# Rewriting a fused S4-convolution, dense-SiLU forward and backward kernel: feature-major FFN with DMA transposes, per-channel SSM columns, data-stationary inverse DFT, natural-layout gradients

## The chip, the cores and the metric

The kernel runs on one core of one Trainium2 chip. Times are microseconds (us) of device time for one execution, as medians over several runs; smaller is better. The profile is one execution of the kernel, and its span differs a little from the median. Engines are named as the profile names them: PE (matmul), PEld (weight load; its busy time overlaps PE's, 161 beside 190 us in the 268 us of SSM forward below), DVE (VectorE), ACT (ScalarE), POOL (GpSimd), SP (the SyncE queue that issues DMAs). An eviction is a copy of a matmul's result from PSUM to SBUF, and a DMA's landing is the arrival of its data, counted here from its issue.

## The reference, cut to what matters

The program computes the forward pass and all gradients of `x + s * g`, with sequence length L = 2048, model width D = 512, state N = 128, FFN width F = 1792, all in bfloat16.

```python
xn = layernorm(x)                                   # [2048, 512]
# branch A: S4 convolution
P  = exp(dt * A * l)                                # [512, 128, 2048], never stored whole
K  = real(einsum("dn,dnl,dn->dl", C, P, dt * B))    # one kernel of 2048 taps per channel
s  = irfft(rfft(xn, 2L) * rfft(K, 2L))[:L] + xn * Dskip
# branch B: gate
g  = silu(silu(xn @ w1) @ w2)                       # [2048, 512] @ [512, 1792] @ [1792, 512]
out = x + s * g
# ... and the gradients with respect to x, A, B, C, log_dt, Dskip, w1, w2, given grad_out
```

Both kernels work in the same stages, whose letters are used below. (A) setup, layernorm, FFN forward and tables of exponentials. (B) SSM forward: the kernel taps K are built from products of these tables, 32 chunks of 16 channels. (C) convolution by DFT on PE, four blocks of 128 channels. (D) backward of FFN and SSM. (E) weight gradients (dW2, dW1) and the last parameter gradients.

## The kernel before: the parts that matter

SSM forward, one chunk (cut): two strided evictions of the taps, with a mask, and a sum of both later; then K goes to DRAM and is read back by the convolution.

```python
ps = psum.tile([P, 8, 32, 2], F32, name="ps_k", tag="ps")
# ... 32 matmuls ...
nc.scalar.activation(out=tmpP[:, 1, :, qa:qa + 8].rearrange("p j q -> p q j"), in_=ps[:, :, :, 1], func=ACT.Copy, scale=k.odd[:, 0:1])
nc.scalar.activation(out=tmpP[:, 0, :, qa:qa + 8].rearrange("p j q -> p q j"), in_=ps[:, :, :, 0], func=ACT.Copy, scale=k.even[:, 0:1])
# ... after all chunks of a block ...
nc.vector.tensor_tensor(out=KF[:], in0=tmpP[:, 0], in1=tmpP[:, 1], op=ALU.add)
```

Inverse DFT (cut): a stage, then PE transposes with their own evictions, then the second stage.

```python
for g0 in range(0, G, 4):
    # ... matmuls with the DFT matrix as the stationary operand ...
    EV(nc, Z[:, c, g0:g0 + 4, :], ps[:])
for c in range(2):
    for g0 in range(0, G, 8):
        # ... 8 PE transposes of Z into pt ...
        EV(nc, dst, src)
# ... second stage ...
```

The FFN backward works token by token and rebuilds what it needs (cut):

```python
for t in range(T):
    # dO of this token tile, transposed on PE (pt_do)
    for fc in range(NFC):
        # ps_h: h again, 4 matmuls; ps_da: 4 matmuls
        nc.scalar.activation(out=a_s[:, fs], in_=ps_h[:], func=ACT.Silu)
        nc.scalar.activation(out=th[:], in_=ps_h[:], func=ACT.Tanh, scale=0.5)
        # ... three DVE operations for silu' ...
        nc.vector.scalar_tensor_tensor(out=dh_s[:, fs], in0=u[:], scalar=1.0, in1=ps_da[:], op0=ALU.add, op1=ALU.mult)
    nc.sync.dma_start(k.Ad[t], a_s[:])
    # ... 14 PE transposes of dh_s (pt_dh), dhT evicted, ps_dx ...
```

The stages follow one another: `gen_half` (tables) beside the FFN forward, then SSM forward, then the convolution, then the backward, then the weight gradients beside the final SSM gradients. DMAs alternate between the queues of SP and ACT.

## Time and profile before

The median is 1345 us (four runs, 1341.65 to 1346.33). The view below gives, for each stretch of the span (us), the busy time of each engine with the number of its instructions, the clock granted to PE, the busy share of the DMA engines and their rate. The stretches are the stages: setup; FFN and tables (A); SSM forward (B); convolution (C); backward (D); weight gradients and finish (E).

```profile
core 0: us, PE busy (x) PEld busy (x) DVE busy (x) ACT busy (x) POOL busy (x), PEclk, DMA share, GB/s
0.00:56.00 56.00, 10.75 (x56) 5.91 (x58) 25.29 (x55) 37.33 (x74) 5.91 (x42) 1.00 0.22 78
56.00:255.00 199.00, 108.32 (x501) 49.44 (x510) 133.85 (x194) 154.81 (x206) 3.45 (x8) 0.80 0.30 109
255.00:523.00 268.00, 190.26 (x2704) 161.04 (x2704) 241.01 (x390) 160.41 (x219) 0.00 (x0) 0.84 0.49 153
523.00:850.00 327.00, 211.96 (x1936) 135.66 (x1956) 202.01 (x220) 186.88 (x299) 0.00 (x0) 0.87 0.27 60
850.00:1170.00 320.00, 243.62 (x1975) 137.04 (x1995) 229.38 (x530) 166.88 (x337) 0.00 (x0) 0.86 0.78 177
1170.00:1348.00 178.00, 128.19 (x1087) 91.47 (x1091) 62.90 (x104) 37.92 (x83) 0.00 (x0) 0.82 0.69 160
```

Read each row for its busiest engine. SSM forward keeps DVE busy 241 of 268 us. The convolution keeps no engine busy for more than 65% of its 327 us: its engines wait for each other much of the time. So a change that runs these two beside each other has room: their DVE sums, for example, are 443 us in 595.

The groups of instructions (line, engine, operation, out<-in, shapes; then busy us and mean ns; then the idle time before them and what ended it) that the change removes or replaces, among others:

```profile
L646 ACT ACTIVATE kf_tmpP<-ps_k,even 128x256 bf16<-128x256 f32 x32 | 51.8, 1619 | 5.5 <-DVE YTf L634 5.5
L645 ACT ACTIVATE kf_tmpP<-ps_k,odd 128x256 bf16<-128x256 f32 x32 | 45.4, 1420 | 78.0 <-PE ps_k L642 76.5 <-PE ps_s_5496 L105 0.8 <-PE pf_t L621 0.6
L770 DVE TENSOR_TENSOR Gbd<-Gt,MK 128x512 bf16<-128x512 bf16 x64 | 43.4, 687 | 37.5 <-PE psV L777 36.0 <-DMA Gt<-dKd 1.5
L902 ACT ACTIVATE b_th<-ps_hb 128x448 bf16<-128x448 f32 x64 | 34.7, 542 | 0.0
```

### The profile page before, as it was taken

How to read it: one execution, taken by the hardware profiler on the slowest of the kernel's cores; microseconds unless marked ns; L12 is line 12 of the kernel's file. 1: busy time of each engine (PE TensorE's matmuls, PEld its weight loads, DVE VectorE, ACT ScalarE, POOL GpSimd, SP SyncE). 2: the span in 40 equal slices, each digit the busy share in tenths (PEclk: the TensorE clock that was granted, in tenths of full speed). 3: DMA queues.
4: the chain of work that ended last, by engine and by line, in shares of the span. 5: the costliest groups of instructions: out<-in, count | busy, mean ns of one | idle time of the engine just before them, and what ended most of it. 6: DMA issues, size and time to landing. Idle time of an engine off the chain costs nothing. (4 is left out here: it accounts for less than half of the span.)

```text
span 1348.3 us, 20797 instructions
## 1 busy us (share of the span) xinstructions
PE 893.1 (66%) x8258; PEld 580.6 (43%) x8314; DVE 894.4 (66%) x1490; ACT 744.2 (55%) x1217; POOL 9.4 (1%) x50
## 2 busy tenths in 40 slices
PE   1486850376767674666676666288788888646997
PEld 0232320266656563334354443144444444333487
DVE  7177877597989894494756748187777777857100
ACT  5779887285646455547475565255555555541111
POOL 0000000000000000000000000000000000000000
PEclk9999985587888887889898888598888898856999
DMA  3112312546463736442411102977686877897744
GB/s 129 59 62 86 133 67 89 206 158 210 125 195 103 204 110 146 97 94 47 94 33 32 32 1 46 221 160 184 150 185 153 178 168 180 156 171 211 176 130 117
DMA packets 333686, 171.90 MB, mean 127 GB/s; under 512 B 287890, under 2 KB 300052, under 8 KB 333076
## 3 DMA queue, kind: packets, MB, share of 16 engines
q1 hardware_dynamic: 179348, 102.65, 28.5%
q10 hardware_dynamic: 154240, 67.91, 20.3%
q8 instruction: 65, 1.06, 0.3%
q14 instruction: 33, 0.27, 0.1%
HBM read 93.19 MB, written 77.33 MB: 126 GB/s over the span
## 5 line engine op out<-in xcount | busy, mean ns | idle before, releaser
L620 PE MATMUL pf_t<-ident_bfloat_87,Xc 128*128 128x128 bf16 x512 | 84.4, 247 | 96.1 <-DVE Xc L344 72.9
L620 PEld LDWEIGHTS <-Xc 128*128 128x128 bf16 x512 | 54.3, 112 | 80.6 <-issue 69.9
L645 ACT ACTIVATE kf_tmpP<-ps_k,odd 128x256 bf16<-128x256 f32 x32 | 45.4, 1420 | 78.0 <-PE ps_k L642 76.5
L622 ACT CAST XTf<-pf_t 128x512 bf16<-128x512 f32 x128 | 74.0, 658 | 26.1 <-PE pf_t L621 12.5
L779 ACT CAST Vb<-psV 128x512 bf16<-128x512 f32 x128 | 67.1, 594 | 29.8 <-PE psV L777 23.3
L621 PE MATMUL pf_t<-ident_bfloat_87,Xc 128*128 128x128 bf16 x512 | 79.3, 245 | 4.2 <-DVE Xc L347 3.5
L922 PE MATMUL ps_dx<-W1T,dhT 128*128 128x512 bf16 x204 | 66.4, 472 | 7.0 <-ACT dhT L184 4.7
L770 DVE TENSOR_TENSOR Gbd<-Gt,MK 128x512 bf16<-128x512 bf16 x64 | 43.4, 687 | 37.5 <-PE psV L777 36.0
L621 PEld LDWEIGHTS <-Xc 128*128 128x128 bf16 x512 | 54.1, 112 | 31.9 <-issue 23.0
L524 PE MATMUL ps_h<-XNT,W_291 128*128 128x512 bf16 x217 | 55.8, 407 | 16.8 <-ACT th L538 9.5
L899 PE MATMUL ps_da<-W2T,DOT_s 128*128 128x448 bf16 x256 | 60.9, 358 | 7.8 <-ACT DOT_s L184 3.7
L633 PE MATMUL pt_t<-ident_bfloat_87,YY 128*64 128x128 bf16 x512 | 49.0, 252 | 23.5 <-DVE YY L331 14.1
L896 PE MATMUL ps_hb<-W_291,XNT 128*128 128x448 bf16 x256 | 60.7, 355 | 3.1 <-ACT Vb L779 1.9
L642 PE MATMUL ps_k<-YY,Xc 128*128 128x64 bf16 x1024 | 48.8, 207 | 15.4 <-ACT kf_tmpP L646 14.8
L646 ACT ACTIVATE kf_tmpP<-ps_k,even 128x256 bf16<-128x256 f32 x32 | 51.8, 1619 | 5.5 <-DVE YTf L634 5.5
L534 PE MATMUL ps_o<-W_440,aT 128*128 128x512 bf16 x220 | 49.8, 379 | 4.8 <-ACT aT L526 4.5
L633 PEld LDWEIGHTS <-YY 128*64 128x64 bf16 x512 | 38.3, 129 | 33.2 <-DVE YY L331 17.5
L777 PE MATMUL psV<-XT,Gbd 128*128 128x256 bf16 x256 | 48.6, 330 | 5.8 <-DVE Gbd L770 2.6
L642 PEld LDWEIGHTS <-Xc 128*128 128x128 bf16 x1024 | 42.8, 107 | 21.2 <-issue 16.9
L974 PEld LDWEIGHTS <-xn 128*128 128x128 bf16 x512 | 48.9, 98 | 4.1 <-issue 2.2
L114 PE MATMUL pt_b<-ident_bfloat_87,dftA 128*128 128x128 bf16 x384 | 31.5, 238 | 28.3 <-ACT dftA L26 14.8
L634 DVE COPY YTf<-pt_t 64x1024 bf16<-64x1024 bf16 x64 | 41.8, 680 | 11.9 <-PE pt_t L633 7.3
(2228 smaller groups left out, 2558.9 us busy)
## 6 DMA issues: line engine op xcount, KB each, us to landing
XTD<-XTf SPq DMA_DIRECT2D x32, 512.0 KB, 3.3
XT<-XTD SPq DMA_DIRECT2D x32, 512.0 KB, 4.3
YTD<-YTf ACTq DMA_DIRECT2D x32, 256.0 KB, 2.9
YT<-YTD SPq DMA_DIRECT2D x32, 256.0 KB, 4.0
YT<-YTD ACTq DMA_DIRECT2D x32, 256.0 KB, 4.8
Ad<-a_s SPq DMA_DIRECT2D x16, 448.0 KB, 3.3
DHd<-dh_s ACTq DMA_DIRECT2D x16, 448.0 KB, 4.3
A_ft<-Ad SPq DMA_DIRECT2D x7, 512.0 KB, 4.0
```

What stands on the lines that cost most here:

```text
L524: nc.tensor.matmul(out=ps[:], lhsT=W1[:, dk, ft * P:(ft + 1) * P], rhs=XNT[:, dk, 4 * tcn:4 * tcn + 4, :], start=(dk == 0), stop=(dk == DK ...
L534: nc.tensor.matmul(out=pso[:], lhsT=aT[:, ft, tt * P:(tt + 1) * P], rhs=W2[:, ft, :], start=(ft == 0), stop=(ft == FT - 1))
L620: nc.tensor.matmul(out=pf[:, qi, c, :], lhsT=X[:, 2 * c, qb + qi].rearrange("p a b -> p (a b)"), rhs=k.ident[:], start=True, stop=False)
L621: nc.tensor.matmul(out=pf[:, qi, c, :], lhsT=X[:, 2 * c + 1, qb + qi].rearrange("p a b -> p (a b)"), rhs=k.ident[:], start=False, stop=True)
L622: nc.scalar.copy(out=XT[:, qb:qb + 2], in_=pf[:])
L633: nc.tensor.transpose(out=pt[0:64, qi, c, :], in_=YY[:, c, qb + qi, 0:32, :].rearrange("p j e -> p (j e)"), identity=k.ident[:])
L642: nc.tensor.matmul(out=ps[:, qi].rearrange("p j e -> p (j e)"), lhsT=X[:, m, q].rearrange("p a b -> p (a b)"), rhs=YY[:, m // 2, q, 32:64, ...
L646: nc.scalar.activation(out=tmpP[:, 0, :, qa:qa + 8].rearrange("p j q -> p q j"), in_=ps[:, :, :, 0], func=ACT.Copy, scale=k.even[:, 0:1])
L779: nc.scalar.copy(out=Vb[:, qb:qb + 2], in_=psV[:])
L896: nc.tensor.matmul(out=ps_h[:], lhsT=XNT[:, dk, t, :], rhs=W1[:, dk, fs], start=(dk == 0), stop=(dk == DK - 1))
L899: nc.tensor.matmul(out=ps_da[:], lhsT=DOT_s[:, dk, :], rhs=W2T[:, dk, fs], start=(dk == 0), stop=(dk == DK - 1))
L922: nc.tensor.matmul(out=ps_dx[:], lhsT=dhT[:, ft, :], rhs=W1T[:, ft, :], start=(ft == 0), stop=(ft == FT - 1))
```

## The change

The intent: keep the FFN feature-major (features on partitions), so that the backward needs no recomputed h; fetch transposed operands by DMA transpose instead of PE; run SSM forward of block b beside the convolution of block b-1; make the data the stationary operand in the inverse DFT, which saves its transposes; sum the SSM gradients with a fixed stationary selector; do the final gradients in natural layout. Nearly the whole file changes; the core, cut:

```diff
 # stage order
-        interleave([gen_half(k), gf], [1, 6])
-        interleave([gen_ssm_fwd(k, (hp, ck)), ffn_then_wT()], [2, 1])
+    interleave([half, gf], [1, 2])
+        run(gen_ssm_fwd(k, 0))
+        for b in range(1, NB):
+            interleave([gen_ssm_fwd(k, b), gen_conv(k, b - 1)], [1, 2])
+        run(gen_conv(k, NB - 1))
 # ...
 # tables: one single-buffered tile T4, its copies on GpSimd
+    T4 = hp.tile([P, 2, HSZ], BF16, name="T4")
+        for h in range(2):
+            nc.gpsimd.tensor_copy(out=vXH[:, h, 0:2, :, :, 1], in_=vXH[:, h, 0:2, :, :, 0])
+            nc.gpsimd.tensor_copy(out=vYL[:, h, :, :, 1]..., in_=vYL[:, h, :, :, 0]...)
+            nc.gpsimd.tensor_copy(out=yh[:, :, 1], in_=yh[:, :, 0])
+            nc.gpsimd.tensor_scalar(out=T4[:, h, OXH + 2048:OYL], in0=T4[:, h, OXH + 1024:OXH + 2048], scalar1=-1.0, ...)
+        nc.sync.dma_start(k.hd[:, 2 * b:2 * b + 2, :], T4[:])
 # ...
 # taps: no mask, no sum, K stays in SBUF
-                nc.scalar.activation(out=tmpP[:, 1, ...].rearrange("p j q -> p q j"), in_=ps[:, :, :, 1], func=ACT.Copy, scale=k.odd[:, 0:1])
-                nc.scalar.activation(out=tmpP[:, 0, ...].rearrange("p j q -> p q j"), in_=ps[:, :, :, 0], func=ACT.Copy, scale=k.even[:, 0:1])
+            for e in range(2):
+                es = slice(64 * e, 64 * e + 64)
+                k.ev_k(KF[es, :, qb:qb + QCH].rearrange("p j q -> p q j"), ps[es, :, e, :])
 # ...
 # dW2 operand, dW1 operand, W1T, W2T, dO: by DMA transpose, all issued on SP
-        (nc.sync if ft % 2 == 0 else nc.scalar).dma_start(A_ft[:], Adv[:, :, ft * P:(ft + 1) * P])
+        nc.sync.dma_start_transpose(out=A_ft[:], in_=k.at_d[ft * P:(ft + 1) * P, :])
+    nc.sync.dma_start_transpose(out=W2T[:], in_=k.ins["B_w2"])
+    nc.sync.dma_start_transpose(out=W1T[:], in_=k.ins["B_w1"])
 # ...
 # FFN backward: u = silu'(h) - 1 was stored by the forward
+            nc.sync.dma_start(u[:], utv[:, f0:f0 + 2, ls])
+                nc.vector.scalar_tensor_tensor(out=dhT[:, ft, :], in0=u[:, s], scalar=1.0, in1=ps[:], op0=ALU.add, op1=ALU.mult)
```

## The prediction

> **What bounds the kernel now.** No single engine: the page gives PE 66%, DVE 66%, ACT 55% of 1348 us. By first and last starts of each tile, and busy time per window, there are five stages. (A) Setup, layernorm, FFN forward and SSM tables: 0 to 255 us; from 178 to 235 us only DVE and ACT work (PE idle in the 200:250 window). (B) SSM forward, 255 to 523 us: 32 chunks of 8.2 us, DVE 90% busy (ten 0.68 us products and two 0.68 us transposed copies each). (C) Convolution, 523 to 850 us: four blocks of 78.6 us with no engine above about 75%, a chain of evictions (ACT 1.02 us and 0.6 us) and products. (D) Backward, 850 to about 1175 us: PE 76%, DVE 72%, DMA 78% busy. (E) Final SSM gradients, dW2, dW1, to 1348 us: the chain shows waits for parameter loads (5 to 10 us each), A_ft loads (4 to 6 us) and small dW1 output stores (56 KB, 1.5 to 5 us each).
>
> **What the change does.**
> - A: the FFN's derivative (tanh, from the same PSUM) moves forward: 56 more ACT evictions of 0.6 us and 28 DVE pairs. The SSM tables now hide under the FFN. ACT sum: FFN about 86 us, tables about 80 us; GpSimd gets 32 copies of 1024 elements, no duration known, on a single-buffered table tile. I expect the SSM stage to start at 250 us, as before.
> - B and C: convolution of block b-1 now runs beside SSM forward of block b. Inverse DFT loses its transposes and their evictions; Dskip folds into one spectrum; K stays in SBUF; products with G move to the FFN tail. All evictions go to ACT. Per merged block I sum DVE 55+30 = 85 us, ACT 46+60 = 107 us (ACT-bound), PE below both (128-column matmul pairs issue every 56 ns). So 60 (first block alone) + 3 x 113 + 75 (last alone) + 10 = about 485 us, against 595.
> - D: backward no longer recomputes h (256 matmuls of 448 columns), nor transposes dh and dO on PE, nor runs silu/tanh and three DVE operations per piece. The Gbd products (64 x 0.69 us) become 8 operations; the 16-byte gradient gathers (Gt, 131072 packets, 76 us of all engines' time) go. The sums use a stationary selector. Per-engine sums with dW2 overlapped: PE about 230 us, DVE 180, ACT 100, DMA about 250 us. I expect 290 us.
> - E: dW1 needs 48 us of PE plus exposed transposed loads; final gradients in natural layout run beside it: 75 us against 175.
>
> The new risk is about 21 MB of DMA transposes, which this trace doesn't contain. [...] The trace's plain 256-byte packets take 18 ns, i.e. about 225 GB/s over 16 engines. At that rate the transposes cost 90 us of DMA time, mostly overlapped.
>
> Sum: 250 + 485 + 290 + 75 = 1100; with 20 us for stage seams, **1120 us**, 80% range 1030 to 1250. Chances: faster 0.92, same 0.04, slower 0.04.
>
> **What would show it.** First SSM product (X) near 250 us; merged blocks 105 to 120 us with ACT above 85% busy; backward from A_ft's first load to the last ps_da/ps_dx under 310 us; each 512 KB transpose under 4 us from issue to landing; dW1 stage PE over 60% busy.
>
> **What would make it wrong.** Transposes at under 100 GB/s or a costly issue on the one SP queue (adds 100 to 200 us in D and E); slow GpSimd copies serialising the tables (adds 50 us in A); the 32-element strided K evictions on ACT costing more than 1.2 us each[...].

Two passages are cut where they are marked: a rate for DMA transposes and a risk about the granted clock. "At that rate" refers to the plain packets: 256 bytes in 18 ns on 16 engines are about 225 GB/s, so 21 MB take some 90 us, an estimate.

## More of the kernel before

An eviction of 256 elements per partition takes 1.4 to 1.6 us here, where one of 448 contiguous elements takes 0.54 us.

## The result, and the profile after

The changed kernel is correct and takes 1193.69 us (median of four runs, 1188.06 to 1197.21) against 1345.38 us of the kernel before: a ratio of 0.887, with a 95% interval of 0.884 to 0.890. Ratios here are the mean time of one kernel's fast runs over that of the other's in the same rounds, so they are not quite the ratios of the medians that are quoted. The prediction of 1120 us had the direction and the range right, and was 74 us too low.

The same view as before, of the kernel after. The stretches are: setup; FFN and tables (A); SSM forward and convolution together (B+C); dW2; backward; dW1 and the finish.

```profile
core 0: us, PE busy (x) PEld busy (x) DVE busy (x) ACT busy (x) POOL busy (x), PEclk, DMA share, GB/s
0.00:45.00 45.00, 17.12 (x137) 10.85 (x138) 36.78 (x112) 23.48 (x28) 15.33 (x62) 1.00 0.48 149
45.00:316.00 271.00, 119.25 (x425) 44.30 (x423) 198.19 (x219) 150.68 (x304) 114.36 (x32) 0.71 0.42 156
316.00:763.00 447.00, 335.40 (x4032) 268.05 (x4032) 308.79 (x468) 383.37 (x592) 0.78 (x1) 0.87 0.43 131
763.00:859.00 96.00, 56.78 (x225) 22.89 (x226) 8.56 (x9) 4.09 (x7) 6.23 (x2) 0.82 0.96 220
859.00:1109.00 250.00, 195.75 (x960) 87.54 (x958) 162.60 (x271) 81.06 (x148) 0.00 (x0) 0.88 0.82 223
1109.00:1186.00 77.00, 50.91 (x256) 25.44 (x256) 29.35 (x48) 7.32 (x13) 0.00 (x0) 0.83 0.61 137
```

Set against the terms of the predicted sum (the measured bounds are tiles in the trace: the first X, which is SSM forward's first product, the end of the last dKs, the convolution's last result, and the end of the last psS, the sums of the SSM gradients; ps_da, used below, is the first matmul of the FFN backward, and UX the first result of a convolution block):

| term | predicted | measured | difference |
|---|---|---|---|
| A, to the first X | 250 | 316.6 | +66.6 |
| B+C, to the last dKs | 485 | 446.2 | -38.8 |
| D, dW2 and backward | 290 | 346.0 | +56.0 |
| E, dW1 and finish | 75 | 77.3 | +2.3 |
| seams | 20 | in the others | -20 |
| sum (span of the profile) | 1120 | 1186.1 | +66.1 |

Two errors of opposite sign stood in the first two terms, and a third in D. The groups that answer to those of before, and the ones that turn out to matter:

```profile
L74 ACT CAST KF<-ps_k 64x256 bf16<-64x256 f32 x64 | 84.6, 1321 | 4.1 <-PE ps_k L564 3.6
L721 DVE TENSOR_SCALAR Gbd<-Gbd,i32c 64x2048 bf16<-64x2048 bf16 x8 | 8.9, 1110 | 10.3 <-DMA Gbd<-dk_d 10.3
L454 POOL COPY T_370<-T_370 128x1024 bf16<-128x1024 bf16 x8 | 62.7, 7841 | 82.2 <-DVE T_370 L60 82.2
L737 PE MATMUL psV<-XT,Gbd 128*128 128x256 bf16 x256 | 48.1, 323 | 40.5 <-DMA XT<-xt_d 40.2 <-ACT Vb L74 0.3
```

The Gbd products went from 43.4 to 8.9 us as intended, and b_th is gone from the backward. The tap evictions kept most of their cost (84.6 us after 45.4 + 51.8). T_370 is the table tile T4, and eight GpSimd copies of it (L454) took 62.7 us, 7.8 us on average. A mean like that hides very different copies, so look at them one by one: GpSimd's timeline (start us, duration us, instruction, and in brackets the idle time before it and what ended it).

```profile
82.51 22.23 POOL L454 COPY T_370<-T_370 128x1024 bf16<-128x1024 bf16 x1 [40.65 <-DVE T_370 L60]
104.68 3.21 POOL L453 COPY T_370<-T_370 128x1024 bf16<-128x1024 bf16 x2
107.80 1.26 POOL L454 COPY T_370<-T_370 128x1024 bf16<-128x1024 bf16 x1
...
141.53 26.79 POOL L454 COPY T_370<-T_370 128x1024 bf16<-128x1024 bf16 x1 [23.97 <-DVE T_370 L60]
168.26 2.89 POOL L453 COPY T_370<-T_370 128x1024 bf16<-128x1024 bf16 x2
171.06 1.04 POOL L454 COPY T_370<-T_370 128x1024 bf16<-128x1024 bf16 x1
```

The same copy, with the same shape, takes 26.79 us and 1.04 us (of the eight, two took over 22 us, one 7.62 us, and five 1.0 to 1.4 us). In that long stretch DVE ran 32 instructions back to back. Here is the end of it on DVE's timeline:

```profile
166.70 0.71 DVE L502 SCALAR_TENSOR_TENSOR cat<-th_1095,Gt 128x512 bf16<-128x512 bf16 x1
167.58 1.15 DVE L60 TENSOR_TENSOR RC<-MG,RC 128x384 f32<-128x384 f32 x1 [0.17 <-ACT RC L423]
```

The first gap in DVE's work since the copy began is the 0.17 us before 167.58, and the copy ended 0.9 us after that gap opened, which is about what a copy takes undisturbed (1.04 us at 171.06, with DVE idle). (In the first case, 82.51 to 104.74, there was no gap; there a DVE product beside the copy's end took 1.27 us where its like takes 0.44.) A busy DVE is not the whole story, though: the copies that followed a long one ran at 1.3 to 1.8 us each with DVE busy beside them (104.68 to 109.06, 205.19 to 209.63), while in the second of these stretches DVE's products of 0.6 us took 1.3 to 1.5 us. So once a copy had got in, both engines went on beside each other, DVE more slowly; why, and why the first of a series waits so long, is not shown. What it does to the rest is plain: the tile has one buffer, so its 4 MB store starts late, and the next tables wait for that store with the FFN's work queued behind them in order. The waits of this stage (engine, line, what it waited for: us in total, times, longest us):

```profile
PE ps_h L478 <- ACT th L482: 75.7, 9, 35.5
DVE T_370 L60 <- DMA hd<-T_370: 38.2, 2, 22.9
```

### The profile page after: what moved, and what is told of

It is laid out like the page before. It is cut to its first block, busy times and chain, and to the rows that moved or that the text cites. A ratio compares the mean times of both kernels' runs of the same rounds, so it can differ in the third digit from the quotient of the medians.

```text
span 1186.1 us, 15777 instructions
## 1 busy us (share of the span) xinstructions
PE 775.2 (65%) x6033; PEld 459.1 (39%) x6033; DVE 744.3 (63%) x1126; ACT 650.0 (55%) x1091; POOL 136.7 (12%) x96
## 5 line engine op out<-in xcount | busy, mean ns | idle before, releaser
L519 DVE TENSOR_TENSOR X<-H 128x1024 bf16<-128x1024 bf16 x128 | 83.8, 689 | 74.5 <-PE ps_k L564 64.6
L540 PE MATMUL pf_t<-ident_bfloat_80,X 128*128 128x128 bf16 x1024 | 93.8, 254 | 49.7 <-ACT KF L74 27.3
L540 PEld LDWEIGHTS <-X 128*128 128x128 bf16 x1024 | 80.3, 116 | 60.7 <-issue 52.6
L74 ACT CAST KF<-ps_k 64x256 bf16<-64x256 f32 x64 | 84.6, 1321 | 4.1 <-PE ps_k L564 3.6
L60 DVE TENSOR_TENSOR T_370<-MG,RC 128x896 bf16<-128x896 f32 (+1 forms) x32 | 49.2, 1615 | 43.0 <-DMA hd<-T_370 38.2
L454 POOL COPY T_370<-T_370 128x1024 bf16<-128x1024 bf16 x8 | 62.7, 7841 | 82.2 <-DVE T_370 L60 82.2
L662 PE MATMUL ps_da<-DOT,W2T 128*128 128x512 bf16 x224 | 57.1, 400 | 0.2
L74 ACT COPY dftB<-pt_b 128x1024 bf16<-128x1024 bf16 x48 | 46.2, 1054 | 3.4 <-PE pt_b L95 3.3
L564 PE MATMUL ps_k<-YY,X 128*128 128x64 bf16 x1024 | 42.7, 203 | 7.1 <-ACT KF L74 6.6
L564 PEld LDWEIGHTS <-X 128*128 128x128 bf16 x1024 | 40.7, 105 | 9.8 <-issue 8.6
L95 PE MATMUL pt_b<-ident_bfloat_80,dftA 128*128 128x128 bf16 x384 | 31.8, 236 | 17.9 <-ACT dftB L74 10.7
L74 ACT COPY YTf<-pt_t 128x1024 bf16<-128x1024 bf16 x32 | 34.6, 1080 | 13.6 <-issue 8.5
```

Source lines behind the costliest of these rows:

```text
L60: nc.vector.tensor_tensor(out=out, in0=a, in1=b, op=ALU.mult)
L74: self.nc.scalar.copy(out=out, in_=in_)
L95: nc.tensor.transpose(out=pt[:, gi, :], in_=A[:, c, g0 + gi, :, :].rearrange("p t e -> p (t e)"), identity=k.ident[:])
L454: nc.gpsimd.tensor_copy(out=vYL[:, h, :, :, 1].rearrange("p c g r l -> p c g (r l)"), in_=vYL[:, h, :, :, 0].rearrange("p c g r l -> p c g ...
L519: nc.vector.tensor_tensor(out=out.rearrange("p (r h l u) -> p r h l u", h=nh, l=4, u=2), in0=h, in1=l, op=ALU.mult)
L540: nc.tensor.matmul(out=pf[:, qi, m // 2, :], lhsT=X[:, m, q + qi], rhs=k.ident[:], start=(m % 2 == 0), stop=(m % 2 == 1))
```

## The experiments

Twelve kernels were run. Runs a, c and d start from the changed kernel (1193.69 us); b, e and f start from the first experiment, which had been found faster.

### a1_tables_act: the table copies on ACT

```diff
-            nc.gpsimd.tensor_copy(out=vXH[:, h, 0:2, :, :, 1], in_=...)      # and the copies of vYL and yh
-            nc.gpsimd.tensor_scalar(out=T4[:, h, OXH + 2048:OYL], in0=..., scalar1=-1.0, ...)
+            nc.scalar.copy(out=vXH[:, h, 0:2, :, :, 1], in_=...)
+            nc.scalar.mul(out=T4[:, h, OXH + 2048:OYL], in_=..., mul=-1.0)
```

> Only the 32 table copies of GpSimd (four per half-block, twice per block) move to ACT; same values, correct result. Theory (GpSimd's copies are starved while DVE is busy: 22.2 and 26.8 us for copies that otherwise take 1.0 to 1.6 us, and the single table tile then stops DVE, ACT and PE in order): the first X starts at about 270 us instead of 316.6 (40 to 50 us earlier), DVE's wait for the table store (38.2 us) falls under 15 us, the total falls by 35 to 50 us to 1145 to 1160. Rival (the single table tile with its 4 MB stores of 11.9 us and the slow strided products of 2.08 us are what serialises, whichever engine copies): first X at 300 us or later, gain under 15 us.

Measured: correct, 1154.26 us (ratio to before 0.858). The first X starts at 276.3 us, 40.3 us earlier; no other stage moved by more than 4 us (the later ones grew a little, so that the profiled span fell by 31.8 us and the median by 39). The rest of the first error, 26 us, stays in this version:

```profile
45.00:276.00 231.00, 121.19 (x418) 44.70 (x423) 179.35 (x220) 183.05 (x336) 0.00 (x0) 0.76 0.49 183
```

DVE is busy 179 of 231 us and ACT 183, of which the moved copies are 38 us. What follows: 40 of the 66.6 us came from the copies standing on GpSimd. That a busy DVE is what holds the first copy up rests on the timing above, 26.79 us beside 32 DVE instructions back to back against 1.04 us with DVE idle; by what mechanism was not measured.

### c1_kf_dve: the tap evictions on DVE

```diff
-    k.ev_k = Evac(nc, 0)     # all on ACT
+    k.ev_k = Evac(nc, 1)     # all on DVE
```

> Only the 64 strided evictions KF<-ps_k (64x256, 1.32 us each on ACT, 84.6 us in all) move to DVE; correct result. Theory (the merged blocks, about 100 us each, are bound by ACT at 92% busy): with 21 us of each block's ACT work gone to DVE (70 to 76% busy) both engines come near 80 us, merged blocks fall to 85 to 92 us, the first block of 74 us falls a little; total 25 to 45 us less. Rival (the block is a chain of waits among PE, ACT and DVE, and order, not ACT's sum, sets it; or DVE pays for the stride as much): blocks stay within 4 us of 100, total within 12 us of 1194, or DVE takes over 1.6 us per eviction and blocks get longer.

Measured: correct, 1197.0 us, no gain. A DVE eviction takes 1.30 us, as long as on ACT. Two merged blocks in this run:

```profile
495.00:595.00 100.00, 73.73 (x973) 59.05 (x975) 92.77 (x125) 73.66 (x128) 0.00 (x0) 0.90 0.47 145
595.00:695.00 100.00, 75.51 (x992) 59.95 (x998) 93.34 (x128) 73.92 (x128) 0.00 (x0) 0.88 0.41 127
```

The bound moved to DVE, 93 of 100 us, where it had been ACT, 91 of 100. My expectation was mis-added: 75 us of DVE's own work and 21 us of evictions make 96, not 80. The run was a poor test of the theory, and it did not tell the two apart.

### d1_plain_loads: what does the transposition cost? (wrong result)

```diff
-        nc.sync.dma_start_transpose(out=A_ft[:], in_=k.at_d[ft * P:(ft + 1) * P, :])
+        nc.sync.dma_start(A_ft[:], plain(k.at_d, ft))    # same bytes, 256-byte rows, not transposed
 # the same for DH
```

> Wrong result on purpose (dW1 and dW2): the 28 transposed loads of A_ft and DH become plain loads of the same bytes in the same 256-byte packets; nothing else changes. Theory (the transposition itself costs little once issued: packets take 18 ns as plain ones do; what costs is the 2.0 to 2.6 us that one takes to issue on SP, 32 us for 14 of them, and the W1T, W2T and DOT transposes left in place): the dW2 stage of 92 us falls to 70 to 80 us, dW1 by 5 to 10 us, total 15 to 30 us less. Rival 1 (the transposition is dear in transfer): landing falls from 4.8 to under 3 us and the total by over 40 us. Rival 2 (it costs nothing, the bytes do): total within 8 us of 1194.

Measured: 1195.73 us, no gain; dW1 and dW2 are wrong, as meant. The line of each kernel's DMA list (queue, kind, count, median us from issue to landing); after:

```profile
A_ft<-at_d SPq DMA_TRANSPOSE x14, 4.8
DH<-dht_d SPq DMA_TRANSPOSE x14, 5.0
```

and with plain loads:

```profile
A_ft<-at_d SPq DMA_DIRECT2D x14, 512.0 KB, 4.4
DH<-dht_d SPq DMA_DIRECT2D x14, 512.0 KB, 5.1
```

From the end of dKs to the first ps_da the stage fell from 96.0 to 88.3 us. The theory had expected 70 to 80. A transpose of A_ft occupies SP for a median of 2.3 us, a plain load for 0.37 us. The finish grew by 12 us: in SP's queue the loads of the SSM sums now stand behind the last DH loads (the first at 1148 us, where the changed kernel had it at 1128), which the edit did not mean to change. So the total falls in the second rival's range partly by accident: it is 8 us gained in one stage and 12 lost in another. What the run does show is that the transposition of A_ft is nearly free, 8 us of the 96 with its issue. That the packets of 256 bytes are what costs was not varied here; b2_hoist_loads and e3_hoist_after_loads below take some of them out of the stage. For the landing it shows no cost either, 4.8 and 5.0 us against 4.4 and 5.1, if the regular load is cut into the same 256-byte packets. The rate that the prediction took from plain packets, about 225 GB/s, was near: the dW2 stage of the changed kernel moved 220 GB/s, other loads included, with its DMA engines 96% busy. Its 51200 packets of 256 bytes took a mean of 20.3 ns, 65 us of all sixteen engines; by themselves they come to about 202 GB/s, an estimate from these two numbers.

### c2_no_overlap: SSM forward and convolution one after the other

```diff
-            for b in range(1, NB):
-                interleave([gen_ssm_fwd(k, b), gen_conv(k, b - 1)], [1, 2])
+            for b in range(NB):
+                run(gen_ssm_fwd(k, b))
+        # ... pools of SSM forward closed, those of the convolution opened ...
+            for b in range(NB):
+                run(gen_conv(k, b))
```

> The SSM forward blocks run all before the convolution blocks again, as in the kernel before, with every removed operation still removed; correct result. Theory (the gain of 140 us in this part comes from running the two beside each other, since the last convolution block alone takes 77 us, hardly less than the 78.6 us of before): first X to the end of the convolution goes from about 451 us to 4 x 72 + 4 x 77 = 596 us, total about 145 us more. Rival (the removed transposes, evictions and reloads made the gain): total at most 60 us more.

Measured: correct, 1265.8 us, 72 us more. Both expectations missed; the truth is between them. First X to the last dKs takes 517 us, against 446 with the overlap and about 595 in the kernel before. So the overlap is worth 71 us, and what was removed or moved elsewhere 78 us. The view also gives the sums of work without overlap, SSM forward first, then the convolution:

```profile
316.00:561.00 245.00, 173.80 (x2325) 149.91 (x2326) 195.58 (x320) 181.36 (x226) 0.00 (x0) 0.78 0.49 171
561.00:834.00 273.00, 196.71 (x1696) 137.99 (x1707) 111.70 (x148) 208.86 (x367) 1.06 (x1) 0.86 0.27 61
```

ACT's work per block is (181.4 + 208.9) / 4 = 97.6 us. The prediction had 46 + 60 = 106. A convolution block alone takes 68 us here (from one UX to the next), where the kernel before took 78.6 us.

### b1_kf_half_tail: half of the tap evictions on DVE, and the last store in rows

```diff
-    k.ev_k = Evac(nc, 0)
+    k.ev_k = Evac(nc, 2)     # every second one on DVE
 # ...
-        nc.sync.dma_start(k.outs[8].rearrange("(k p) -> p k", p=P), ddt_b[:])
+    nc.tensor.transpose(out=pt[0:DK, :], in_=ddt_b[:], identity=k.ident[:])
+    nc.vector.tensor_copy(out=ddt_r[:], in_=pt[0:DK, :])
+    nc.sync.dma_start(k.outs[8].rearrange("(k p) -> k p", p=P), ddt_r[:])
```

> Two edits in stages that do not touch, on top of the kernel of run a1_tables_act (1154 us): (1) every second KF eviction goes to DVE instead of all of them (32 of 64, 42 us); (2) the last store, ddt_b as 512 two-byte writes (16.0 us from issue to landing), becomes a PE transpose and a store of four rows. Correct result. Theory for (1) (merged blocks are bound by the busiest engine; with all evictions on ACT that was ACT at 91 of 100 us, with all on DVE it was DVE at 93): split evenly, ACT and DVE have about 81 and 84 us per block, and merged blocks fall from 100 to 87 to 93 us, so first X to the end of the last dKs goes from 449 to 412 to 430 us. Rival (a chain of waits between PE, ACT and DVE sets the block, the busy shares only follow): blocks stay at 98 to 101 us. For (2): the gap between the last DVE instruction and the end falls from 18 us to under 7 us; if the 16 us are not due to the small writes, it stays above 14 us. Total 1105 to 1125 us if both hold.

Measured: correct, 1141.14 us, 13 us less, all of it from the store. From ddt_b to the end it is 3.2 us instead of 17.9; in the changed kernel this one DMA of 1 KB showed

```profile
L60 DVE TENSOR_TENSOR ddt_b<-ddt,n_dtb x1: 164/164/164, 1168.5 to 1168.5; 128x4 bf16<-128x4 f32 x1
L833 SPq DMA_DIRECT2D out_dram<-ddt_b x1: 382/382/382, 1168.7 to 1168.7; - x1
...
DMA to landing us min/median/max: 16.0/16.0/16.0
```

and the kernel ended with it: 512 writes of two bytes.

Merged blocks took 100.7 us with ACT busy 83 and DVE 85 of 100 us, against 102.7 and 105.5 in a1_tables_act. So the simple theory of the busiest engine fell. But the split was not clean either. In most chunks DVE's half waits for ACT's half of the same tile: 25 of 32 times in all, and in one merged block (453 to 553 us; us in total, times, longest):

```profile
DVE KF L72 <- ACT KF L74: 4.0, 6, 1.4
```

One chunk on the timeline (here DVE was busy with a product until 483.64):

```profile
481.88 1.43 ACT L74 CAST KF<-ps_k 64x256 bf16<-64x256 f32 x1
483.67 1.31 DVE L72 CAST KF<-ps_k 64x256 bf16<-64x256 f32 x1
```

The two still stand one after the other for about 3 us, and part of PE's next pf_t waits for the second. So the pair of evictions of a chunk had not become shorter, although PE's waits for it did: over the run, 17.6 us against 37.0 in a1_tables_act.

### e1_kf_read_order: the same eviction, walked the other way

```diff
-                k.ev_k(KF[es, :, qb:qb + QCH].rearrange("p j q -> p q j"), ps[es, :, e, :])
+                k.ev_k(KF[es, :, qb:qb + QCH], ps[es, :, e, :].rearrange("p q j -> p j q"))
```

The store in rows of b1_kf_half_tail is in it too. The evictions are all on ACT.

> On top of a1_tables_act (1154 us), with the tail store of b1_kf_half_tail (known: 15 us less): the KF evictions all stay on ACT, but walk their 64x256 elements in the other order, so that the writes to SBUF are runs of 8 neighbours and the jumps are in the reads from PSUM. Correct result. Theory 1 (the 1.32 us come from writing with a 128-byte stride): one eviction falls to 0.4 to 0.7 us, ACT loses 40 to 55 us in all, and since all four blocks wait for ACT the stretch from first X to the last dKs (449 us) falls by 25 to 45 us. Theory 2 (order costs nothing, or jumps in the reads cost as much): 1.2 us or more each, stretch unchanged. Theory 3 (evictions get cheap but the block is a chain of waits, as the split in b1_kf_half_tail, 446 us with ACT at 83 and DVE at 88 of 100 us, suggests): evictions under 0.7 us and the stretch within 10 us of 449.

Measured: correct, 1086.33 us, 68 us less than a1_tables_act, of which 15 us are the known store.

```profile
L74 ACT CAST KF<-ps_k 64x256 bf16<-64x256 f32 x64 | 24.8, 387 | 2.5 <-PE ps_k L564 2.1
```

An eviction takes 387 ns instead of 1322. ACT lost 59.8 us, and the stretch from first X to the last dKs fell by 54.3 us, from 448.9 to 394.6 (a little more than expected). Two merged blocks of about 90 us:

```profile
422.00:512.00 90.00, 72.67 (x998) 57.66 (x1001) 76.63 (x117) 79.05 (x148) 0.00 (x0) 0.96 0.56 170
512.00:602.00 90.00, 73.63 (x1000) 58.51 (x1003) 71.55 (x108) 79.38 (x148) 0.00 (x0) 0.96 0.49 145
```

So the cost was the order of the writes to SBUF, steps of 128 bytes, and not the number of elements: 1322 ns with these steps, 387 ns with runs of eight bf16 neighbours. Jumps of 256 bytes in the reads from PSUM, which came with it, did not cost anything like that: the 387 ns are for 256 elements with these jumps, beside 595 ns for 512 contiguous ones (Vb, in the same run). Why steps in the writes cost so much was not measured. Open remains whether the 54 us came from ACT's sum of work or from the shorter wait of each chunk for its two evictions: the edit shortens both, and b1_kf_half_tail, meant to tell them apart, did not separate them.

### b2_hoist_loads: transposed loads during the last convolution block

```diff
+    # buffers of SSM forward closed before the last convolution block; in their place:
+        k.wt = wt.enter_context(tc.tile_pool(name="wt", bufs=1, side="right"))
+        load_wt(k)                     # A_ft of ft = 0 to 4, W2T, W1T, by DMA transpose on SP
         run(gen_conv(k, NB - 1))
```

> On top of a1_tables_act: the buffers of SSM forward are closed before the last convolution block, and in their place W1T, W2T and the first five A_ft tiles are loaded by DMA transpose during that block, whose DMA engines are 24% busy. Correct result. Theory (the dW2 stage, 93 us long with its DMA engines 98% busy while its 224 matmuls need about 48 us of PE, is bound by the 51200 packets of 256 bytes of these transposes, 65 us of all 16 engines): 24576 of these packets leave the stage, 30 us of the engines, and the stretch from the last dKs to the first ps_da falls from 98 us to 60 to 72 us; the last convolution block stays within 4 us of its length; total 1118 to 1132 us. Rival (the stage is a chain of load latencies, 4.8 us each with two buffers; or the convolution pays for the DMA): the stretch falls by under 15 us, or the last block grows by over 10 us.

Measured: correct, 1149.98 us, 4 us less. The dW2 stage fell as expected, from 97.6 to 65.4 us, but the last convolution block grew from 69 to 94 us. SP's timeline shows why:

```profile
657.64 13.28 SPq L237 DMA_TRANSPOSE A_ft<-at_d  x5
670.96 7.10 SPq L239 DMA_TRANSPOSE W2T<-in_B_w_dram  x1
678.10 7.18 SPq L240 DMA_TRANSPOSE W1T<-in_B_w_dram  x1
685.33 2.27 SPq L606 DMA_DIRECT2D cat_b<-cat_d  x2
```

The block's own input cat_b stood behind 27.6 us of transposes in the queue.

### e3_hoist_after_loads: the same, behind the block's own loads

```diff
-        load_wt(k)
-        run(gen_conv(k, NB - 1))
+        gc = gen_conv(k, NB - 1)
+        for _ in range(4):
+            next(gc)
+        load_wt(k)
+        run(gc)
```

> As b2_hoist_loads, but the transposes stand after the last convolution block's own loads in SP's queue (there cat_b waited 28 us behind them and the block grew from 69 to 94 us). Correct result. Theory: the stretch from last dKs to first ps_da stays at about 65 us as in b2_hoist_loads (98 without the hoist) and the last block is back to 69 to 76 us, total 1122 to 1132 us. Rival (the block pays for DMA traffic beside it, not for the order): it stays over 85 us and the total above 1140 us.

Measured: correct, 1124.3 us, 30 us less, as expected. The last block takes 69 us, the dW2 stage 65.1 us; the backward grew by 7.5 us. So it was the order in the queue that made the last block longer before, not traffic: the same transposes run beside it here, at a DMA share of 0.66 where a1_tables_act had 0.19 in the same 69 us. The dW2 stage lost 32.5 us with 24576 of its 51200 packets, about 31 us of the sixteen engines at the mean of 20.3 ns that they took in the changed kernel. Five A_ft buffers instead of two came with that, but the engines were 95% busy in the stage before and 99% after, so it is their throughput that bounds it.

### b3_xt_on_act_queue and b4_three_buffers: the waits for XT in the backward

```diff
 # b3
-                nc.sync.dma_start(XT[:], ...)          # and YT
+                nc.scalar.dma_start(XT[:], ...)
 # b4
-                XT = bp.tile([P, 2, 4, 2, P], BF16, name="XT", tag="XT")            # and YT
+                XT = bp.tile([P, 2, 4, 2, P], BF16, name="XT", tag="XT", bufs=3)
```

> On top of a1_tables_act: the loads of XT and YT in the backward stage are issued from ACT's DMA queue, all else stays on SP's. Correct result. Theory 1 (one in-order SP queue holds these loads back behind stores that wait for DVE: PE waits 40 us for XT in this stage of 251 us, SP waits about 75 us for DVE and ACT): PE's wait for XT falls under 15 us and the stage from first ps_da to last psS falls by 20 us or more to below 231 us. Theory 2 (the DMA engines, 82% busy, and the landing of 4.5 us set it, whichever queue issues): the stage stays within 8 us of 251 us. Theory 3: issuing 160 loads costs ACT so much that Vb comes later: the stage gets longer by 5 us or more.

> On top of a1_tables_act: XT and YT in the backward stage get three buffers instead of two, all queues as they are. Correct result. Theory 1 (prefetch depth: a load can only be issued when the tile of two chunks before is free, and then lands 4.5 us later): PE's wait for XT falls under 15 us, the stage of 251 us falls by 15 us or more. Theory 2 (SP's order or the DMA engines' throughput sets it): within 6 us of 251 us.

Measured: both correct; 1151.82 us and 1151.3 us, within 3 us of their base. On ACT's queue PE's wait for XT did fall, as theory 1 had it, from

```profile
PE psV L737 <- DMA XT<-xt_d: 39.5, 13, 6.4
```

to

```profile
PE psV L737 <- DMA XT<-xt_d: 8.5, 5, 3.0
```

and the stage got 7 us longer (258.0 against 250.8): the waits turned up at the products instead (PE's wait for them grew from 14.4 to 31.9 us). From the last dKs to the end nothing changed, 428.9 against 429.1 us, since the first matmuls of dW1 now start before the last psS. With three buffers the wait stayed (42.2 us) and the stage took 247.3 us. So shortening the wait that was named did not shorten the whole. Theory 2's range held in both, but b3_xt_on_act_queue also falls in theory 3's, 5 us longer or more: ACT's evictions Vb now waited 41.3 us in all behind the YT loads in ACT's own queue. So it is no clean test of the queue.

### e2_no_xt_traffic: the backward without its loads (wrong result)

```diff
-                XT = bp.tile(...); nc.sync.dma_start(XT[:], ...)               # and YT
+                if c == 0:                                                      # one chunk of eight
+                    XT = bp.tile(...); nc.sync.dma_start(XT[:], ...)
```

> Wrong result on purpose (the SSM gradients): on top of a1_tables_act, XT and YT are loaded for the first of the eight chunks of each block only and used for all, so 7 of 8 of these loads and of their 1024- and 2048-byte packets are gone; every instruction of PE, DVE and ACT stays. Theory 1 (the backward stage, 251 us with the DMA engines 84% busy and PE waiting 40 us for XT, is bound by these loads): the stage from first ps_da to last psS falls to under 220 us. Theory 2 (PE, at 193 of 250 us busy with weight loads beside it, and the products between are the bound, and the waits for XT are only slack of one queue that a third buffer or another queue turned into other waits): the stage stays above 238 us. Either way the dW2 stage (98 us) may lose up to 8 us, since the first loads run beside it.

Measured: 1088.82 us, 65 us less than a1_tables_act; the SSM gradients are wrong, as meant. The stage from first ps_da to last psS takes 199.3 us instead of 250.8; the other 14 us came off the finish, where dW1 again starts before the last psS. In a1_tables_act it was

```profile
823.00:1074.00 251.00, 194.05 (x944) 87.49 (x958) 162.22 (x271) 81.33 (x148) 0.00 (x0) 0.89 0.83 222
```

and without the loads

```profile
819.00:1019.00 200.00, 186.35 (x966) 84.85 (x981) 160.54 (x271) 81.04 (x149) 0.00 (x0) 0.98 0.54 144
```

The instructions of PE, DVE and ACT are the same (PE's busy time fell by 8 us, at a granted clock of 0.98 instead of 0.89); the DMA share fell from 0.83 to 0.54, and PE became the bound with 186 of 200 us. So the loads of XT and YT bounded the backward: theory 1 held. That it is their throughput, with the engines 83% busy, is argued: a third buffer did not help, so it is not the depth of prefetch alone, but this edit also took the loads' issues off SP's queue, and b3_xt_on_act_queue was no clean test of that. The packets of the changed kernel's backward say where it goes: 34944 packets of 1024 bytes at a mean of 59 ns are 129 us of all sixteen engines, 8064 of 2048 bytes at 102 ns are 51 us. The 1024-byte ones are YT, u and dhT above all.

### f1_combined: the four edits that held

The copies on ACT, the eviction's order, the store in rows, and the hoisted loads behind the block's own.

> The four edits that held, together: table copies on ACT, KF evictions in the other order, transposed loads of W1T, W2T and five A_ft tiles behind the loads of the last convolution block, and the four-row store at the end. Correct result. If their gains lie in separate stages, they add: 1086 us (copies, KF order, store) less the 30 us that the hoist gave, 1050 to 1062 us. Rival (the shorter convolution leaves the DMA engines less time, so the hoisted loads run into the last block or are given back in the backward stage, which is bound by DMA): 1068 us or more.

Measured: correct, 1062.22 us (five runs, 1058.33 to 1065.55), just above the upper end of what adding gave. Its ratio to the kernel before is 0.789 (0.786 to 0.792). Stage by stage: first X at 277.3, 395.4 us to the last dKs, 66.4 us for dW2, 258.3 us of backward, 66.2 us to the end. By medians it is 24 us faster than e1_kf_read_order, where the hoist alone had given 30. In the two profiled executions the dW2 stage is 29 us shorter, and the backward takes back 10 us of it.

## Why the prediction was right or wrong

**Direction and range: right.** The gain was predicted for the overlap of SSM forward and convolution and for the work removed there. The experiment without the overlap splits it into 71 us and 78 us. That the total lay well inside the range is partly luck: A and D were together 123 us longer than predicted, and B+C and the seams, which were too high, took back 59 of that.

**A, "I expect the SSM stage to start at 250 us, as before": wrong by 66.6 us.** The step that failed is "GpSimd gets 32 copies of 1024 elements, no duration known, on a single-buffered table tile", counted as free. Undisturbed they take 1 to 3 us; one, beside a DVE without gaps, took 26.8 us, and everything behind the single buffer waited. Moving them gave back 40 us. The prediction's list of what would make it wrong had "slow GpSimd copies serialising the tables (adds 50 us in A)". It was right to name it and wrong to leave it out of the sum. The other 26 us are not tested. It may be that A's sum counted ACT alone (86 + 80 us) while DVE had 198 us to do in 271; among its work are 32 products into strided tables, 1.6 us each.

**B+C, "60 + 3 x 113 + 75 + 10": too high by 39 us.** ACT was the busiest engine of the merged blocks, as predicted; that its sum of work alone sets their length is not shown (in b1_kf_half_tail ACT fell from 92 to 83 us in 100, and the blocks got only 2 to 5 us shorter). Measured were about 67 us for the first block, 104 for each merged one (ACT 91% busy) and 67 for the last. Three merged blocks make 27 of the 39 us, and the mis-sized term in them is the ACT work of a convolution block, 60 us predicted and 52 us measured; the last block and the 10 us added make the rest, less 7 us by which the first was longer. The named risk "strided K evictions on ACT costing more than 1.2 us each" also came true, at 1.32 us. Had the evictions been cheap, by the 54 us of e1_kf_read_order, the term would have been too high by about 93 us.

**D, "DMA about 250 us. I expect 290 us": too low by 56 us.** DMA was listed as the largest sum and then treated as something that overlaps. Measured in the changed kernel it is 0.96 x 96 + 0.82 x 250 = 297 us of busy engines, in 346 us. So the sum was 47 us too small, and the step that failed beside it is "At that rate the transposes cost 90 us of DMA time, mostly overlapped". The cost was about right, 65 us in dW2 and about 35 for DH, but not the overlap: in the dW2 stage the DMA engines were 96% busy and PE 57 of 96 us, and moving 24576 of the packets away took off 32.5 us. In the backward 51.5 us go with the XT and YT loads. The claim of under 310 us for the backward (from the first A_ft load to the last ps_dx: 316) missed for the same reason, and so did "each 512 KB transpose under 4 us" (4.8 and 5.0). That last miss is not due to transposition, since plain loads in such packets landed in 4.4 and 5.1.

**"a costly issue on the one SP queue (adds 100 to 200 us in D and E)": the issue was costly, the effect small.** A transpose holds SP for 2.3 us, but plain loads saved only 8 us in the dW2 stage, and a second queue for XT and YT left the time as it was.

**E, 75 us: right,** at 77.3 us with PE busy 66% ("over 60%"). Two errors cancelled in it. The prediction had 48 us of PE and some 27 us of exposed loads; the trace shows 6 us of exposed load before 51 us of matmuls, and then a tail of 18 us that the prediction did not see, the last store in two-byte pieces.

## What to carry to other kernels

When a sum of work names the largest term, do not ask that the resource be at 100% before it counts as the bound: here a stage with its DMA engines 83% busy got 51 us shorter when loads were taken out, and a wait that the profile names (PE for XT) shrank from 39.5 to 8.5 us without the time moving. For a slow eviction, look at the step of its writes before moving it to another engine (1322 ns with steps of 128 bytes, 387 without); turning the walk around was worth 54 us, moving all of it nothing and half of it 3 us. Be wary of a short copy on GpSimd beside a busy DVE when a single-buffered tile depends on it (one took 26.8 us instead of 1.0; 40 us in all here), and of ending a kernel with a store in single elements (15 us here).
